# Window attention and a SoLU feed-forward block: plain float32 products of the first tiles from unsplit weights, and a start cut into halves

## The chip, the core and the metric

The kernel runs on one core of a Trainium2 chip. It is measured in microseconds of device time; the figure before the change is the median of three runs, 604.48 us (603.85 to 604.65). The engines are named as in the profile: PE multiplies matrices (PEld is its loading of the stationary operand), DVE, ACT and POOL work elementwise, and SP only issues transfers here.

## What is computed

The reference has two parts. Attention: 8 batches, 8 heads, 576 positions, 64 columns a head; every position sees itself and the 63 before it.

```python
scores = scale * np.matmul(q, k.transpose(0, 1, 3, 2))
mask = (rel >= 0) & (rel < window)              # window = 64
attn = softmax of the masked scores             # sum + 1e-9 below
x = np.matmul(attn, v)                          # 4608 tokens x 512
```

The feed-forward block on these 4608 rows, with `w_in` 512x1024 and `w_out` 1024x512:

```python
h = x @ w_in
sm = softmax(h)
solu = h * sm
ln = (solu - mean) / np.sqrt(var + 1e-6) * g_ln
out = ln @ w_out
```

The two weights are drawn as float64 (8 bytes a number), so the kernel reads 4 MB for each and turns the pairs of 32-bit words into float32 itself.

## The kernel before

The tokens are cut into 36 tiles of 128. For each tile `t` the work is the same:

- `load` (L296 to L317): q, k and two halves of v come in by transfers that SP issues.
- `scores` (L322 to L344): 16 small float32 products on PE into `pS`. `softmax` (L346 to L373): eight DVE operations add the mask and find the maxima, eight ACT operations take the exponential (`sS`, sums in `sm`), DVE makes reciprocals, and POOL multiplies the eight heads (L371).
- `transposes` (L378 to L394): eight PE transposes into `t`, copied to `PT` by ACT (first four heads) and DVE (the others).
- `values` (L405 to L419): 16 small float32 products into `pX`. ACT copies `pX` to `xH` in a reduced float32 format (fp32r), and DVE writes the rest, `xL = pX - xH`.
- `moe_in` (L429 to L437): `pH = x @ w_in` in two column halves. Each 128x512 product is made of three in fp32r: `xH*w_inH`, `xH*w_inL` and `xL*w_inH`, so 12 PE products a half and 24 a tile. There is one `pH` buffer, so the products of tile `t+1` wait until the norm of tile `t` has read it.
- `moe_norm` (L439 to L473): a maximum on DVE (L449), exponential on ACT (L451), product and sum on DVE (L454), square on ACT (L460), small columns on DVE and POOL, and two scalings of `e` on POOL (L471).
- `moe_transpose` and `moe_out` (L481 to L516): eight transposes of `e`, the copies `yH` and `yL`, 24 products into `pO` in the same three-part form, a copy to `ot` and a transfer out.

Before use, each of 16 blocks of weights, 128x512 each, is decoded (`weight_block`, L234 to L270): a transfer of 512 KB into `raw`, one ACT operation (L256), four DVE operations (L257, L259, L261, L263), for `w_out` a scaling by `g` on POOL (L266), a copy to the high part on ACT (L268), and the subtraction for the low part on POOL (L269). In the names of the trace `wt` is the block being decoded.

No engine chooses its order at run time. The functions above only record operations in a `Plan`, each with an engine, an estimated cost, what it reads and what it writes. `Plan.order` (L99 to L145) gives every operation a due time from the order in which PE's work was recorded, and then builds one list: at each step the engine that can begin first takes, of its ready operations, the one that is due first. Buffers are rings (`RINGS`, L33): an operation on buffer `n` waits for all users of the one that had its place. The order of PE is exactly the recorded order. The recording at the end of the function sets it: first the loads and weights of the start, then for each `t` the products of tile `t`, the transposes of `t+1`, the scores of `t+3` (`AHEAD`) and the output products of `t-3` (`BEHIND`).

Of the kernel before, what the change touches and what calls it, by code (L numbers as in the profile page):

```python
# [17 lines left out]
P = 128  # L18
# [8 lines left out]
BEHIND = 3  # L27

URGENT = 300
# [4 lines left out]
    "raw": 4, "wt": 3, "q": 3, "k": 3, "v0": 4, "v1": 4, "sS": 3, "PT": 2, "xH": 2, "xL": 2,  # L34
# [5 lines left out]
class Plan:  # L40
# [55 lines left out]
    def order(self):  # L96
# [32 lines left out]
        while any(waiting.values()):  # L129
# [21 lines left out]
def tile_window_attention_solu_moe(  # L151
# [15 lines left out]

    nc = tc.nc
# [9 lines left out]
    NTILE = NT // P  # L178
    SCALE = 1.0 / math.sqrt(D)
# [54 lines left out]
    def weight_block(i, src, wH, wL, g, key):  # L234


        n = wH.shape[-1]

        def raw():
            return T("raw", i, [P, n, 2], I32)  # L240

        def t():
            return T("wt", i, [P, n], I32)

        def tf():
# [9 lines left out]
        plan.dma(P * n * 8, lambda: nc.sync.dma_start(raw().rearrange("p n w -> p (n w)"), src), [], [R])
        plan.op("ACT", 600, lambda: nc.scalar.activation(tf(), hi().bitcast(F32), AF.Abs), [R], [W])  # L256
        plan.op("DVE", 420, lambda: nc.vector.tensor_scalar(  # L257
            tf(), tf(), EXP_LO, EXP_HI, ALU.max, ALU.min), [W], [W])
        plan.op("DVE", 420, lambda: nc.vector.tensor_scalar(  # L259
            t(), t(), 0x07FFFFFF, 3, ALU.bitwise_and, ALU.logical_shift_left), [W], [W])  # L260
        plan.op("DVE", 680, lambda: nc.vector.scalar_tensor_tensor(  # L261
            t(), hi(), -0x40000000, t(), ALU.bitwise_and, ALU.bitwise_or), [R, W], [W])
        plan.op("DVE", 680, lambda: nc.vector.scalar_tensor_tensor(  # L263
            t(), lo(), 29, t(), ALU.logical_shift_right, ALU.bitwise_or), [R, W], [W])
# [4 lines left out]
        plan.op("POOL", 1300, lambda: nc.gpsimd.tensor_sub(wL, tf(), wH.bitcast(F32)),  # L269
                [W, ("H", *key)], [("L", *key)])  # L270
# [321 lines left out]
```

## Time and profile before

| | us |
|---|---|
| median of three runs | 604.48 |
| the profiled execution, whole | 604.69 |
| its span (first to last instruction) | 602.5 |
| PE busy in the span | 563.9 |
| DVE busy | 322.0 |
| ACT busy | 313.3 |
| POOL busy | 210.2 |
| PE busy from 0 to 20 us | 1.98 |
| PE busy from 100 to 500 us | 400.0 |

The whole execution is 2.19 us longer than the span. In the tables by stretch, the first number behind the stretch is its length, and then come the busy time of PE, PEld, DVE, ACT and POOL with the number of instructions, the granted clock of PE, the busy share of the transfer engines and GB/s. In a timeline row the first number is the start, the second how long it took; what stands in brackets is how long the engine had been idle before, and what it waited for. Matmuls overlap, so the distance between two starts, not the length of one, is what a product costs PE. In the chain of waits the second number is the time that a piece adds to the chain.

### The profile page before, as it was taken

To read this page: it belongs to the slowest core of one execution; us is meant where nothing else is said; L and a number is where in the kernel's file an instruction comes from. 1 tells how busy PE (TensorE), PEld (TensorE's weight loads), DVE (VectorE), ACT (ScalarE), POOL (GpSimd) and SP (SyncE) were. 2 spreads that over 40 slices of the span, in tenths; PEclk is the share of its full clock that TensorE was granted. 3 is DMA by queue.
4 is the path that set the end of the run, shared out by engine and by line. 5 is a ranking of instruction groups with operands and counts; after the bars stand their busy time and mean duration, and the time that the engine had idled before them with its cause. 6 is when DMAs were issued, how large, how long until landed. Compare 5 with 4: busy or idle time off the path is not lost.

```text
span 602.5 us, 12551 instructions
## 1 busy us (share of the span) xinstructions
PE 563.9 (94%) x4608; PEld 459.3 (76%) x4608; DVE 322.0 (53%) x1180; ACT 313.3 (52%) x933; POOL 210.2 (35%) x438
## 2 busy tenths in 40 slices
PE   1387699999999999999999999999999999999997
PEld 1256578888888888888888888888888888888775
DVE  6768997555555555555555555555555555554430
ACT  3467666555555555555555555555555555553421
POOL 4554668333333333333333333333333333331110
PEclk9988889999999999999999999999999999999999
DMA  8882753333333333333333333333333331000000
GB/s 296 254 262 93 204 157 95 92 91 97 93 95 98 95 97 97 94 93 96 89 98 97 96 97 97 97 97 97 97 97 97 97 97 54 18 18 18 18 36 35
DMA packets 56204, 60.97 MB, mean 101 GB/s; under 512 B 3408, under 2 KB 40272, under 8 KB 56144
## 3 DMA queue, kind: packets, MB, share of 16 engines
q1 hardware_dynamic: 56144, 60.18, 32.7%
q8 instruction: 36, 0.59, 0.4%
q14 instruction: 24, 0.20, 0.1%
HBM read 50.73 MB, written 9.44 MB: 100 GB/s over the span
## 4 chain that ended last, share of the span: by engine, by line
PE 90%; DVE 5%; ACT 2%; POOL 1%; DMA 1%; issue 1%; SPq 0%; ACTq 0%
PE pO L508 35%; PE pH L434 34%; PE pX L411 6%; PE t L387 6%; PE pS L340 5%; PE t L491 5%; DVE wt L261 1%; DMA raw<-w_in 1%; DVE wt L263 1%; DVE sS L353 1%; DVE e L454 1%; POOL sS L371 1%; ACT sS L358 1%; POOL w_inL L269 0%; DVE wt L259 0%
## 5 line engine op out<-in xcount | busy, mean ns | idle before, releaser
L371 POOL TENSOR_SCALAR sS<-sS,rec 128x128 f32<-128x128 f32 x288 | 105.0, 386 | 258.6 <-PE pO L508 257.1
L358 ACT ACTIVATE sS<-sS,nmx 128x128 f32<-128x128 f32 x288 | 112.3, 391 | 52.9 <-DVE nmx L353 52.9
L434 PE MATMUL pH<-w_inH,xH 128*128 128x512 f32 x288 | 119.2, 414 | 8.6 <-DVE mst L454 8.6
L508 PE MATMUL pO<-w_outH,yH 128*128 128x512 f32 x288 | 117.7, 409 | 1.2 <-ACT yH L495 1.2
L434 PE MATMUL pH<-w_inH,xL 128*128 128x512 f32 x288 | 116.3, 404 | 0.0
L434 PE MATMUL pH<-w_inL,xH 128*128 128x512 f32 x288 | 116.0, 403 | 0.0
L508 PE MATMUL pO<-w_outH,yL 128*128 128x512 f32 x288 | 114.3, 397 | 0.0
L508 PE MATMUL pO<-w_outL,yH 128*128 128x512 f32 x288 | 113.9, 395 | 0.0
L495 ACT CAST yH<-t 128x512 fp32r<-128x512 f32 x72 | 38.7, 589 | 101.6 <-PE t L491 101.6
L449 DVE TENSOR_REDUCE mst<-pH 128x1 f32<-128x1024 f32 x36 | 44.1, 1224 | 70.5 <-PE pH L434 70.5
L392 DVE COPY PT<-t 128x512 f32<-128x512 f32 x36 | 24.9, 691 | 89.5 <-PE t L387 89.5
L434 PEld LDWEIGHTS pH<-w_inH,xH 128*128 128x128 f32 x288 | 55.3, 192 | 21.0 <-DVE mst L454 5.8
L471 POOL TENSOR_SCALAR e<-e,mst 128x512 f32<-128x512 f32 x72 | 54.9, 769 | 41.3 <-DVE mst L468 39.9
L508 PEld LDWEIGHTS pO<-w_outH,yH 128*128 128x128 f32 x288 | 54.1, 188 | 18.5 <-ACT e L451 4.8
L434 PEld LDWEIGHTS pH<-w_inH,xL 128*128 128x128 f32 x288 | 55.4, 192 | 13.5 <-DVE xL L418 0.2
L508 PEld LDWEIGHTS pO<-w_outH,yL 128*128 128x128 f32 x288 | 54.1, 188 | 14.6 <-DVE yL L497 1.7
L434 PEld LDWEIGHTS pH<-w_inL,xH 128*128 128x128 f32 x288 | 55.5, 193 | 11.7
L508 PEld LDWEIGHTS pO<-w_outL,yH 128*128 128x128 f32 x288 | 54.2, 188 | 11.6 <-POOL w_outL L269 0.2
L392 ACT COPY PT<-t 128x512 f32<-128x512 f32 x36 | 21.1, 585 | 76.5 <-PE t L387 76.5
L353 DVE CUSTOM_DVE_ANT_0 sS<-pS,maskNone 128x128 f32<-128x128 f32 x224 | 51.3, 286 | 14.0 <-PE pS L340 14.0
L387 PE MATMUL t<-ident,sS 128*128 128x128 f32 x288 | 42.0, 283 | 12.9 <-POOL sS L371 12.7
L358 ACT ACTIVATION_READ_ACCUMULATOR sS<-sS,nmx 128x1 f32 x288 | 53.9, 187 | 0.0
(54 smaller groups left out, 722.1 us busy)
## 6 DMA issues: line engine op xcount, KB each, us to landing
v<-vS SPq DMA_DIRECT2D x64, 256.0 KB, 4.1
k<-kT SPq DMA_DIRECT2D x35, 384.0 KB, 4.0
q<-qT SPq DMA_DIRECT2D x36, 256.0 KB, 4.6
y<-ot SPq DMA_DIRECT2D x36, 256.0 KB, 2.0
raw<-w_in SPq DMA_DIRECT2D x8, 512.0 KB, 5.2
raw<-w_out SPq DMA_DIRECT2D x8, 512.0 KB, 5.2
v<-vS SPq DMA_DIRECT2D x16, 128.0 KB, 4.5
k<-kT SPq DMA_DIRECT2D x1, 256.0 KB, 7.8
```

The source lines that it names most:

```text
L340: nc.tensor.matmul(PS(t)[half * WIN:(half + 1) * WIN, r, p], q[rs, p, half * WIN:(half + 1) * WIN], keys, start=True, stop=True)
L353: plan.op("DVE", 215, lambda h=h: nc.vector.tensor_tensor_reduce(SS(t)[:, h], PS(t)[:, h % 2, h // 2], mk, scale=-SCALE, scalar=BIG, op0=A ...
L358: plan.op("ACT", 390, lambda h=h: nc.scalar.activation(SS(t)[:, h], SS(t)[:, h], AF.Exp, bias=cols("nmx", h), scale=-1.0, accum_out=cols(" ...
L371: plan.op("POOL", 360, lambda h=h: nc.gpsimd.tensor_scalar(SS(t)[:, h], SS(t)[:, h], rec()[:, h:h + 1], 0.0, ALU.mult, ALU.add), [("rec", ...
L387: nc.tensor.transpose(pA()[:, i], SS(t)[:, 4 * x + i], ident)
L392: (nc.vector.tensor_copy if x else nc.scalar.copy)(PT(t)[:, 4 * x:4 * x + 4], pA()),
L411: nc.tensor.matmul(PX(t)[r * D:(r + 1) * D, p, ks], V(t, half)[:, h * D:(h + 1) * D], PT(t)[:, h, ks], start=True, stop=True)
L434: plan.op("PE", 233, lambda c=c, k=k, x=x, w=w: nc.tensor.matmul(PH(t)[:, hs], x(t)[:, c], w[:, c, hs], start=(c == k == 0), stop=(c == NC ...
L449: plan.op("DVE", 1150, lambda: nc.vector.tensor_reduce(nmax(), PH(t), axis=AX.X, op=ALU.max, negate=True), [("pH", t)], [key(0)])
L471: plan.op("POOL", 770, lambda h=h, hs=hs: nc.gpsimd.tensor_scalar(E(t)[:, hs], E(t)[:, hs], nmean(), kk(), ALU.add, ALU.mult), [key(4), ke ...
L495: plan.op("ACT", 560, lambda hs=hs, pT=pT: nc.scalar.copy(YH(t)[:, hs], pT()), [("t", n)], [("yH", t, h)])
L508: plan.op("PE", 233, lambda f=f, k=k, y=y, w=w: nc.tensor.matmul(PO(), y(t)[:, f], w[:, f], start=(f == k == 0), stop=(f == NF - 1 and k = ...
```

## The change

The weights of the first tiles are no longer split before they are used.

- Products. For tiles 0 to 2 `moe_in` multiplies `xH`, now a plain float32 copy of `pX`, by the decoded but unsplit weights `w` in plain float32: 8 products a tile, one per 128-row chunk and column half, in place of 24. For tile 0 `moe_out` does the same with `w_out`, 8 products. Tile 3 is the first to use split weights in `moe_in` (`PLAIN_IN`), tile 1 in `moe_out` (`PLAIN_OUT`); the split (`split`) is recorded there. `xL` and `yL` of the plain tiles fall away.
- Weights. They come in 8 chunks of 128x1024 (1 MB of raw words) with one set of decoding operations each; the first chunk comes as two halves. A chunk of `w_in` now holds both column halves of 128 rows, so the first products need the first chunk alone. The scaling by `g` moves from POOL to ACT, and the subtraction for the low part from POOL to DVE. Decoded chunks and low parts share a ring `w` of 9 places: a low part takes the place of a decoded chunk whose users are done.
- Attention of the first tiles. The scores are recorded as two operations of two head pairs each; for tile 0 the reciprocals come in two halves and the eight multiplications are on DVE, not POOL. For tiles 0 to 2 both copies to `PT` are on ACT (`EARLY`), and `values` and the copy to `xH` come in halves.
- Order. `BEHIND` goes from 3 to 2, with the `e` ring (`BEHIND + 1`) following. SP's transfers keep the recorded order, as PE's work does (`last`), except that operations of tile 0 marked `loose` may move on PE. q and k of tile 0 are recorded first. The planner's costs of transfers and weights change, and it adds 90 ns between dependent operations of one engine other than PE. `URGENT`, which nothing used, goes.

```diff
 AHEAD = 3
-BEHIND = 3
+HASTE = 1
+LOOSE = 1
+BEHIND = 2
+EARLY = 3
+PLAIN_IN = 3
+PLAIN_OUT = 1
...
-    "raw": 4, "wt": 3, "q": 3, "k": 3, "v0": 4, "v1": 4, "sS": 3, "PT": 2, "xH": 2, "xL": 2,
+    "raw": 3, "w": 9, "q": 3, "k": 3, "v0": 3, "v1": 3, "sS": 3, "PT": 2, "xH": 2, "xL": 2,
...
-            if engine == "PE":
-                if pe is not None:
-                    before[i].setdefault(pe, False)
-                pe = i
+            if engine in last and not loose:
+                if last[engine] is not None:
+                    before[i].setdefault(last[engine], False)
+                last[engine] = i
...
+        for x in (0, 1) if i == 0 else (slice(0, 2),):
+            n = 512 if i == 0 else 1024
...
         if g is not None:
-            plan.op("POOL", 700, lambda: nc.gpsimd.tensor_scalar(
-                tf(), tf(), g, 0.0, ALU.mult, ALU.add), [W, ("g",)], [W])
-        plan.op("ACT", 600, lambda: nc.scalar.copy(wH, tf()), [W], [("H", *key)])
-        plan.op("POOL", 1300, lambda: nc.gpsimd.tensor_sub(wL, tf(), wH.bitcast(F32)),
-                [W, ("H", *key)], [("L", *key)])
+            for x in range(2):
+                plan.op("ACT", 600, lambda x=x: nc.scalar.mul(tf()[:, x], tf()[:, x], g(x)),
+                        [("g",), W], [("w", i, x)])
...
+    def split(i):
+        for x in range(2):
+            plan.op("ACT", 600, lambda x=x: nc.scalar.copy(WH(i, x), W32(i)[:, x]),
+                    [("w", i), ("w", i, x), ("w", NC + 1 if i < NC else NW - 1)], [("H", i, x)])
+            plan.op("DVE", 620, lambda x=x: nc.vector.tensor_sub(
+                WL(i)[:, x], W32(i)[:, x], WH(i, x).bitcast(F32)),
+                [("w", i), ("w", i, x), ("H", i, x)], [("w", NW + i, x)])
...
+        if t < PLAIN_IN:
+            for c in range(NC if h == 0 else 0):
+                for x in range(2):
+                    plan.op("PE", 930, lambda c=c, x=x: nc.tensor.matmul(
+                        PH(t)[:, x * 512:(x + 1) * 512], XH(t)[:, c], W32(c)[:, x],
+                        start=(c == 0), stop=(c == NC - 1)),
+                        [("xH", t, c // 2), ("w", c), ("w", c, x)], [("pH", t)])
+            return
...
+    load(0, range(2))
+    prep(0)
     scores(0)
     softmax(0)
+    load(0, range(2, 4))
+    prep(1)
     load(1)
+    prep(2)
     transposes(0)
     scores(1)
     softmax(1)
     values(0)
+    prep(3)
     load(2)
...
+            if t - BEHIND == PLAIN_OUT:
+                for i in range(NC, NC + NF // 2):
+                    split(i)
+            on(moe_out, t - BEHIND)
```

How PE begins. Before: scores of tile 0, its transposes, scores of tile 1, values of tile 0, scores of tile 2, then the three-part products of the first column half.

```order
L340 MATMUL pS_158<-k_133,q_141 64x128 x16
L387 MATMUL t_231<-ident,sS_176 128x128 x4
L387 MATMUL t_245<-ident,sS_176 128x128 x4
L340 MATMUL pS_252<-k_155,q_204 64x128 x16
L411 MATMUL pX_274<-PT_239,v_0_221 64x64 x2
...
L340 MATMUL pS_321<-k_250,q_292 64x128 x16
L434 MATMUL pH_342<-w_inH,xH_306 128x512
L434 MATMUL pH_342<-w_inL,xH_306 128x512
L434 MATMUL pH_342<-w_inH,xL_313 128x512
```

Now, at the same place (`w_148`, `w_185`, `w_268` and `w_286` are the four chunks of `w_in`):

```order
L371 MATMUL pS_117<-k_112,q_110 64x128 x16
L425 MATMUL t_187<-ident,sS_134 128x128 x4
L425 MATMUL t_201<-ident,sS_134 128x128 x4
L449 MATMUL pX_210<-PT_199,v_0_138 64x64 x2
...
L371 MATMUL pS_220<-k_176,q_172 64x128 x16
L481 MATMUL pH_240<-w_148,xH_229 128x512 x2
L449 MATMUL pX_210<-PT_199,v_0_138 64x64 x2
...
L481 MATMUL pH_240<-w_185,xH_229 128x512 x2
L481 MATMUL pH_240<-w_268,xH_229 128x512 x2
L481 MATMUL pH_240<-w_286,xH_229 128x512 x2
```

The first chunk's products now stand between the two halves of tile 0's values, and the scores of tile 2 behind the last chunk.

The same stretch on ACT, where the weights' first operation (L279, out of `raw`) stands among the exponentials (L391) and the two copies of tile 0's `xH` (L459):

```order
L391 ACTIVATE sS_134,sm_142<-sS_134,nmx_135 128x128 x4
L279 ACTIVATE w_185<-raw_155 128x1024
L430 COPY PT_199<-t_187 128x512
L430 COPY PT_199<-t_201 128x512
L459 COPY xH_229<-pX_210 128x256
L391 ACTIVATE sS_242,sm_249<-sS_242,nmx_243 128x128
L459 COPY xH_229<-pX_210 128x256
L391 ACTIVATE sS_242,sm_249<-sS_242,nmx_243 128x128
L279 ACTIVATE w_268<-raw_207 128x1024
L391 ACTIVATE sS_242,sm_249<-sS_242,nmx_243 128x128 x5
L279 ACTIVATE w_286<-raw_247 128x1024
```

Before, the copies to `w_inH` of the first four blocks stood ahead of tile 0's exponentials; now no such copy stands in this stretch, and the third chunk (`w_268`) comes behind the second copy of `xH`, which waits for PE.

Where PE's output products begin. Before, the first product of `pO` comes behind the fourth tile's `pH` (`pH_811`, tile 3):

```order
L434 MATMUL pH_811<-w_inH,xH_793 128x512
...
L491 MATMUL t_889<-ident,e_482 128x128 x4
...
L340 MATMUL pS_926<-k_667,q_683 64x128 x16
L508 MATMUL pO_951<-w_outH,yH_903 128x512
```

Now it comes behind the third tile's `pH` (`pH_574`, tile 2), in plain float32, and the products of tile 3 (`pH_760`) follow it:

```order
L481 MATMUL pH_574<-w_286,xH_567 128x512 x2
L425 MATMUL t_617<-ident,sS_423 128x128 x4
...
L549 MATMUL t_633<-ident,e_366 128x128 x4
...
L371 MATMUL pS_671<-k_522,q_505 64x128 x16
L570 MATMUL pO_698<-w_315,yH_640 128x512 x2
L570 MATMUL pO_698<-w_354,yH_640 128x512 x2
L570 MATMUL pO_698<-w_480,yH_640 128x512 x2
L570 MATMUL pO_698<-w_551,yH_640 128x512 x2
L492 MATMUL pH_760<-w_inH,xH_684 128x512
```

From there to the end each `t` has the same sequence on PE as before, with output products one tile nearer. After the last `pH` (tile 35) three output tiles follow, where four did before.

More of the change, by code (lines that the diff above doesn't have):

```diff
@@ L326, in scores, with emit @@
         first = first_of(t)
-        def emit():
+        def emit(ps=range(NPAIR)):
             q, k = Q(t), K(t)
-            for p in range(NPAIR):
+            for p in ps:
                 for half in range(2):
@@ L364, in rec @@
             return T("rec", t, [P, H], pool=st)
[L366 to L373 removed]
+        engine, v, cost = ("POOL", nc.gpsimd, 360) if t else ("DVE", nc.vector, 150)
+        n = H if t else H // 2
+        for o in range(0, H, n):
+            s = slice(o, o + n)
+            R = ("rec", t, o)
+            plan.op("DVE", 130, lambda s=s: nc.vector.tensor_scalar_add(
+                rec()[:, s], T("sm", t, [P, H], pool=st)[:, s], 1e-9),
+                [("sm", t, h) for h in range(o, o + n)], [R])
+            plan.op("DVE", 130, lambda s=s: nc.vector.reciprocal(rec()[:, s], rec()[:, s]), [], [R])
+            for h in range(o, o + n):
+                plan.op(engine, cost, lambda h=h: v.tensor_scalar(
+                    SS(t)[:, h], SS(t)[:, h], rec()[:, h:h + 1], 0.0, ALU.mult, ALU.add),
+                    [R], [("sS", t, h)])
     def PT(t):
@@ L387, in emit @@
                     nc.tensor.transpose(pA()[:, i], SS(t)[:, 4 * x + i], ident)
-            plan.op("PE", 430, emit, [("sS", t, 4 * x + i) for i in range(4)], [("t", n)])
+            plan.op("PE", 430, emit, [("sS", t, 4 * x + i) for i in range(4)], [("t", n)], loose=t < LOOSE)
             plan.op(
-                "DVE" if x else "ACT", 600, lambda x=x, pA=pA:
-                (nc.vector.tensor_copy if x else nc.scalar.copy)(PT(t)[:, 4 * x:4 * x + 4], pA()),
+                "DVE" if x and t >= EARLY else "ACT", 600, lambda x=x, pA=pA:
+                (nc.vector.tensor_copy if x and t >= EARLY else nc.scalar.copy)(PT(t)[:, 4 * x:4 * x + 4], pA()),
                 [("t", n)], [("PT", t, x)])
@@ L404, in values, with emit @@
     def values(t):
-        def emit():
-            for p in range(NPAIR):
+        def emit(ps=range(NPAIR)):
+            for p in ps:
                 for half in range(2):
@@ L413, in emit @@
                             PT(t)[:, h, ks], start=True, stop=True)
-        plan.op("PE", 1100, emit, [("PT", t, x) for x in range(2)]
-                + [(f"v{half}", t, x) for half in range(2) for x in range(2)], [("pX", t)])
+        vals = [(f"v{half}", t, x) for half in range(2) for x in range(2)]
+        if t < PLAIN_IN:
+            for x in range(2):
+                ps = slice(2 * x, 2 * x + 2)
+                plan.op("PE", 550, lambda x=x: emit((2 * x, 2 * x + 1)), [("PT", t, x)] + vals, [("pX", t, x)],
+                        loose=t < LOOSE)
+                plan.op("ACT", 360, lambda ps=ps: nc.scalar.copy(XH(t)[:, ps], PX(t)[:, ps]),
+                        [("pX", t, x)], [("xH", t, x)])
+            return
+        plan.op("PE", 1100, emit, [("PT", t, x) for x in range(2)] + vals, [("pX", t)])
         plan.op("ACT", 560, lambda: nc.scalar.copy(XH(t), PX(t)), [("pX", t)], [("xH", t)])
@@ L494, in moe_transpose @@
             plan.op("PE", 430, emit, [("e", t, h)], [("t", n)])
+            if t < PLAIN_OUT:
+                plan.op("DVE" if h else "ACT", 600, lambda h=h, hs=hs, pT=pT:
+                        (nc.vector.tensor_copy if h else nc.scalar.copy)(YH(t)[:, hs], pT()),
+                        [("t", n)], [("yH", t, h)])
+                continue
             plan.op("ACT", 560, lambda hs=hs, pT=pT: nc.scalar.copy(YH(t)[:, hs], pT()),
```

194 lines of the change are left out of this document (108 added, 86 removed).

## The prediction

> **What bounds the kernel now.** I read the page first, then busy time by stretch, then the chain of waits, and last the timelines of the stretch that turned out to matter. The page's slices (40 of 15 us) and the stretches:
>
> ```profile
> span 602.5 us, 12551 instructions
> PE   1387699999999999999999999999999999999997
> DVE  6768997555555555555555555555555555554430
> ```
> ```profile
> 0.00:20.00 20.00, 1.98 (x32) 1.61 (x32) 14.55 (x35) 8.38 (x19) 8.88 (x22) 1.00 0.89 287
> 20.00:40.00 20.00, 12.89 (x125) 8.31 (x126) 15.32 (x52) 12.18 (x46) 11.31 (x20) 1.00 0.82 251
> 40.00:60.00 20.00, 17.00 (x173) 13.35 (x172) 13.96 (x41) 11.71 (x36) 10.33 (x20) 0.83 0.40 138
> 60.00:80.00 20.00, 14.36 (x108) 11.34 (x109) 18.48 (x61) 13.34 (x44) 13.78 (x18) 0.85 0.80 240
> 206.50:221.75 15.25, 15.25 (x130) 12.59 (x129) 7.74 (x31) 8.15 (x25) 4.86 (x11) 1.00 0.32 96
> ```
>
> PE is full from the sixth slice on, one tile taking 15.25 us with DVE and ACT half idle. Nothing there can be hidden better. Time is lost before 90 us, where DVE, at 14.6 and 18.5 of 20 us, is the busier engine. The chain says what PE did there (the second number is the time added):
>
> ```profile
> 44.47 1.10 PE pX L411 x32
> 48.95 4.51 PE pH L434 x12
> 76.08 4.45 PE pH L434 x12
> 85.30 1.08 PE pX L411 x32
> 86.38 1.03 PE pS L340 x32
> 87.41 5.80 PE pO L508 x24
> 93.21 2.80 PE pH L434 x12
> 96.02 0.87 PE t L387 x8
> ```
> ```profile
> 11.39 1.98 PE L340 MATMUL pS<-k,q 64*64 64x128 f32 x32 [11.39 <-DMA q<-qT]
> 32.80 0.50 PE L434 MATMUL pH<-w_inH,xH 128*128 128x512 f32 x1
> 41.28 0.63 PE L434 MATMUL pH<-w_inH,xH 128*128 128x512 f32 x1
> 41.70 0.63 PE L434 MATMUL pH<-w_inL,xH 128*128 128x512 f32 x1
> 48.95 0.50 PE L434 MATMUL pH<-w_inH,xH 128*128 128x512 f32 x1 [2.36 <-DVE mst L454]
> ```
>
> At 93.21 us PE has done `pO` of tile 0, `pH` of tiles 0 to 3 (5.60 each), `pX` and `t` of five tiles and `pS` of seven: 5.80 + 22.4 + 5.4 + 4.35 + 7.2, and 0.87 for `t` of `e`, 46.0 us. So 47.2 us are lost, in three ways. PE's first product of `pH` starts at 32.80, behind the weights. After each `pH` PE waits until the norm's L454 has read it (2.36 us idle at 48.95). And after such gaps come stretches at 0.43 us a product (41.28 to 41.70) in place of 2.80/12 = 0.233, with the granted clock at 0.83.
>
> **The change, part by part.** First the plain product, which the trace does not show at this size. The nearest rows are `pS` and `pX`, which are float32. Each is 16 products in the code, but 32 records, two per product, where the three-part products have one. From below, two records at 0.233 are 0.47 us. From above: `pS` has 64x64 operands, so four can lie side by side, 1.03/4 = 0.26 per 128 columns, and 1.03 for 512. `pX` (two side by side) gives 1.08/8 = 0.135 per 64 columns; the line through both gives 0.99 for 512. Small shapes carry more fill, so I take 0.95, near the upper rows: 7.6 us for eight products against 5.60, 2.0 more for each of three `pH` and one `pO`.
>
> The Trainium skill, "FP8 and Floating Point Precision", section TensorE Precision Notes, says that true FP32 takes four passes through the array. An estimate by it is 4 x 0.233 = 0.93, and the sum would be 0.5 us shorter; the two records per product don't contradict it.
>
> Now the weights and DVE. Durations, minimum, median and maximum:
>
> ```profile
> L256 ACT ACTIVATE wt<-raw x16: 650/666/697, 4.0 to 78.6; 128x512 f32<-128x512 f32 x16
> L257 DVE TENSOR_SCALAR wt<-wt x16: 418/424/1178, 4.7 to 82.3; 128x512 f32<-128x512 f32 x16
> L259 DVE TENSOR_SCALAR wt<-wt x16: 376/427/882, 5.2 to 83.2; 128x512 int32<-128x512 int32 x16
> L261 DVE SCALAR_TENSOR_TENSOR wt<-raw,wt x16: 680/693/1778, 5.6 to 84.1; 128x512 int32<-128x512 int32 x16
> L263 DVE SCALAR_TENSOR_TENSOR wt<-raw,wt x16: 676/691/1730, 6.4 to 87.6; 128x512 int32<-128x512 int32 x16
> L269 POOL TENSOR_TENSOR w_inL<-wt,w_inH x8: 1264/1288/1407, 7.9 to 39.7; 128x512 fp32r<-128x512 f32 x8
> ```
> ```profile
> 44.51 1.23 DVE L449 TENSOR_REDUCE mst<-pH 128x1 f32<-128x1024 f32 x1 [2.81 <-PE pH L434]
> 46.83 0.28 DVE L353 CUSTOM_DVE_ANT_0 sS<-pS,maskNone 128x128 f32<-128x128 f32 x1
> 47.03 0.29 DVE L353 CUSTOM_DVE_ANT_0 sS<-pS,maskNone 128x128 f32<-128x128 f32 x1
> 47.66 1.22 DVE L454 CUSTOM_DVE_ANT_0 e<-pH,e 128x1024 f32<-128x1024 f32 x1
> 48.12 0.40 ACT L358 ACTIVATE sS<-sS,nmx 128x128 f32<-128x128 f32 x1
> 48.50 0.40 ACT L358 ACTIVATE sS<-sS,nmx 128x128 f32<-128x128 f32 x1
> ```
>
> A half block costs DVE 2.4 us with the gaps. For a 1024-wide chunk the bounds are twice the 512 medians, 4.5, and the 1.22 of L454 for the last two with half as much for the first two, 3.7; I take 4.0. DVE gains 16 subtractions (0.68, like L261) and tile 0's eight multiplications (0.2, between mask and half a half block), 12.5 us; it loses the stretching to 1.7 us that L261 and L263 show at their maximum, as long as L269 on POOL, which is gone.
>
> ```profile
> 0.73 1.81 SPq L255 DMA_DIRECT2D raw<-w_in  x4
> 3.11 0.67 SPq L300 DMA_DIRECT2D q<-qT  x1
> 4.02 0.66 ACT L256 ACTIVATE wt<-raw 128x512 f32<-128x512 f32 x1 [2.02 <-DMA raw<-w_in]
> ```
>
> q and k, now issued first, land some 3.3 us behind an issue at 0.73 and 1.4 (the first `raw` took that): 5.2, not 11.39. At 287 GB/s the chunks land at about 6, 8, 12, 18 and 21 us, always ahead of DVE. From there, in the new order:
>
> - `pS` of tile 0, at half pace, 5.2 to 7.2; eight masks at 0.21 to 8.1; the first chunk's halves (4.8), tile 0's reciprocals (0.8) and multiplications (1.6) on DVE to 15.3; transposes, copies, the first half of `pX` and `pS` of tile 1 to 18.7; first-chunk products, partly at half pace, 20.9; the other half of `pX` 22.0.
> - DVE has chunk 2 at 19.5. Its chunk 3 waits for L279 on ACT, which is queued behind the second `xH` copy (22.5) and an exponential: 24.0, then 4.0 each and 0.4 for reciprocals, so chunk 3 at 28.0 and chunk 4 at 32.4. The last two plain products end at 35.0, partly at half pace.
> - Gap 1: L449 to 36.3, tile 2's masks 1.7, two weight operations 1.5, L454 to 40.8. PE has `pS`, `t`, `pS`, `pX` inside, 4.0 us. `pH` of tile 1: 40.8 + 7.6 + 1.7 for one slow stretch (7 or 8 products at 0.2 more, as around 41 us) = 50.1.
> - Gap 2: L449, two weight operations, L454 to 54.3, the `xH` copy behind weights on ACT to 54.9. `pH` of tile 2: 54.9 + 7.6 + 1.7 = 64.2.
> - L449 and the `PT` copy on DVE 66.1, `pX` and `pS` 68.2, `pO` of tile 0 to 75.9. One more for POOL's multiplications beside DVE, as L257's maximum of 1.18 shows: 76.9.
>
> At that point PE owes one `pH`, `pS`, `t` and `pX` more than at 93.21 before (the output comes one tile earlier): 5.60 + 1.03 + 0.87 + 1.08 = 8.58. Its equal is 84.63, so the start gains 84.63 - 76.9 = 7.7 us. The split casts and subtractions behind it (eight of each, 5 us, against 7 idle us a tile on both engines) are covered by `pO` and `pH`; uncovered they would cost that 5 us.
>
> `BEHIND` also shortens the end:
>
> ```profile
> 584.08 1.04 PE L491 MATMUL t<-ident,e 128*128 128x128 f32 x8
> 591.37 1.03 PE L491 MATMUL t<-ident,e 128*128 128x128 f32 x8
> 219.93 1.52 POOL L471 TENSOR_SCALAR e<-e,mst 128x512 f32<-128x512 f32 x2 [1.33 <-DVE mst L468]
> ```
>
> Output tiles there take 7.29 for 0.87 + 5.80 of work: 0.62 of waiting each, three times and not four. In the steady tiles `e` of the tile whose `pH` ended at 206.5 is ready at 221.5; its transposes come two periods behind 206.5, at 237, so 15 us are left. Sum: 602.5 - 7.7 - 0.6 = 594.2. The profiled execution is 2.19 longer than its span and 0.21 above the median: 594.2 + 2.19 - 0.21 gives 596.2 us, 1.4% faster.
>
> **Rivals.**
>
> - *DVE's floor.* From 6.3 on DVE owes, until tile 3: chunks 33, masks of five tiles 8.5, norms 3 x 3.4, `w_in` subtractions 5.4, tile 0's 2.4, small ones 3, about 62: 68. For it: PE's work to there is 45 us, and slow stretches may fail to come. Against it: DVE waits for PE at three places above. Time 596.2 - 8.9 = 587.3.
> - *DVE held by POOL.* Multiplications on POOL beside 28 weight operations; if eight stretch by 1.0 as L261 did, the start ends at 85: 604. For it: the maxima; against it: those came beside L269, which is gone.
> - *A slow feed.* 512-byte rows of q, k and v delay the chunks, since three, not four, `raw` buffers (of 1 MB) hold SP back: 251 GB/s puts chunk 4 three us later and with the wait two more, 601.
> - *Half pace throughout (slower).* The plain products are spread over gaps. If `pH` of tiles 1 and 2 and `pO` of tile 0 all run at 0.43/0.233 of their time, 24 x 0.95 x 0.85 = 19.4 less the 3.4 counted, 16.0 more: 612.2. It decides from five slow stretches more than I count (8.3 us). For it: four slow stretches between 40 and 81 us; against it: each lasted about 3 us though PE idled between.
>
> The Trainium skill, "TensorE: Matmul & The Clock Gate", section "The HAM clock gate", has the clock halve after an idle window of about 3.4 us. The 2.36 us gap here was enough to be followed by a slow stretch, so the trace disagrees in size; by the page's figure both counted stretches (3.4 us) would fall away.
>
> **How the numbers follow.** Forecast 0.50, DVE's floor 0.22, POOL 0.13, slow feed 0.07, half pace 0.08. The plain product's bounds move 24 products on the path: at 1.03 by +1.9, at 0.47 by -11.5, which DVE's floor stops at 587.3. The range holds that floor and the slow feed, and leaves out the half pace and the upper half of POOL's case: 586.5 to 603.5. About 0.2% (1.2 us) is what a measurement here can tell from no change. Faster 0.86 (forecast, floor, feed, half of POOL), same 0.05, slower 0.09.
>
> **What would show it.** `pS` of tile 0 near 5, a first plain `pH` product near 19, the four chunks' products spread to about 35, `pO` of tile 0 ahead of tile 3 and ending near 77, two records per plain product 0.47 apart, a steady tile still 15.25, and three output tiles after the last `pH`. Wrong would be: idle PE ahead of `t` of `e` in steady tiles, a chunk's L279 waiting for its transfer, or slow plain products in all three batches.

## The result, and the profile after

The changed kernel takes 594.17 us (median of four runs, 593.86 to 595.72), the kernel before 604.57 beside it (603.85 to 605.14): a ratio of 0.9839, with a 95% interval of 0.9824 to 0.9854, or 1.6% faster. The prediction was 596.2. The profiled execution took 593.86, its span 592.1, 10.4 less than the 602.5 before.

The page of the kernel after, span and slices (40 of 14.8 us), answers to the first rows shown of before:

```profile
span 592.1 us, 12478 instructions
PE   2689899999999999999999999999999999999997
DVE  4889985554444444554444455555455555554330
```

The stretches of the kernel after (columns as before: length, busy PE, PEld, DVE, ACT, POOL, the granted clock, transfer share, GB/s):

```profile
0.00:20.00 20.00, 8.29 (x90) 5.96 (x91) 11.06 (x42) 8.41 (x24) 3.62 (x18) 1.00 0.90 304
20.00:40.00 20.00, 14.50 (x136) 7.34 (x134) 16.36 (x48) 11.06 (x31) 5.11 (x8) 0.83 0.84 294
40.00:60.00 20.00, 18.82 (x109) 9.49 (x110) 19.12 (x59) 19.28 (x55) 13.60 (x19) 1.00 0.69 204
60.00:80.00 20.00, 17.98 (x123) 12.32 (x122) 18.50 (x52) 17.33 (x53) 7.68 (x11) 0.91 0.25 74
206.50:221.75 15.25, 15.25 (x130) 12.57 (x129) 7.82 (x32) 8.27 (x26) 4.86 (x11) 1.00 0.32 94
```

PE is full from the sixth slice on, as before, but has 2, 6, 8 and 9 tenths in the first four slices where it had 1, 3, 8 and 7. A steady tile still takes 15.25 us of nothing but PE. Between 40 and 60 us DVE is busy for 19.1 of 20 and ACT for 19.3: the gaps there are filled on three engines at once. Of the chain of waits the output products and the end:

```profile
67.49 7.06 PE pO L570 x16
84.00 5.81 PE pO L580 x24
...
560.87 5.64 PE pH L492 x24
...
582.31 6.14 PE pO L580 x24
```

`pO` of tile 0 ends at 67.49 + 7.06 = 74.55. The equal point before was 84.63, so the start gains 10.1; behind it come 592.1 - 74.55 = 517.55 us, with three output tiles behind the last `pH`. The start on PE, from the timeline (start, length, in brackets the idle time before and what ended it; a plain product has two records):

```profile
4.93 1.98 PE L371 MATMUL pS<-k,q 64*64 64x128 f32 x32 [4.93 <-DMA k<-kT]
17.47 1.99 PE L371 MATMUL pS<-k,q 64*64 64x128 f32 x32
19.39 1.98 PE L481 MATMUL pH<-w,xH 128*128 128x512 f32 x4
...
27.94 6.41 PE L481 MATMUL pH<-w,xH 128*128 128x512 f32 x8 [4.04 <-DVE w L287]
40.06 7.13 PE L481 MATMUL pH<-w,xH 128*128 128x512 f32 x16 [0.47 <-ACT xH L459]
52.61 7.10 PE L481 MATMUL pH<-w,xH 128*128 128x512 f32 x16 [0.58 <-ACT xH L459]
59.55 1.04 PE L425 MATMUL t<-ident,sS 128*128 128x128 f32 x8
61.17 0.63 PE L549 MATMUL t<-ident,e 128*128 128x128 f32 x4 [0.59 <-ACT PT L430]
63.24 0.63 PE L549 MATMUL t<-ident,e 128*128 128x128 f32 x4 [1.43 <-DVE PT L430]
63.79 1.98 PE L449 MATMUL pX<-PT,v 128*64 128x64 f32 x32
65.70 1.79 PE L371 MATMUL pS<-k,q 64*64 64x128 f32 x32
```

Tiles 1 and 2 run at full pace: eight plain products in 7.1 us. The slow places are others: the third and fourth chunk of tile 0 (6.41 for four products), and `pX` and `pS` at 63.8 (1.98 and 1.79, where 1.15 and 1.10 are usual). And ahead of `pO` PE waits twice for copies to `PT`, one on ACT, one on DVE. DVE at that place:

```profile
60.15 1.21 DVE L287 SCALAR_TENSOR_TENSOR w<-raw,w 128x1024 int32<-128x1024 int32 x1
61.28 1.21 DVE L507 TENSOR_REDUCE mst<-pH 128x1 f32<-128x1024 f32 x1
62.42 0.67 DVE L430 COPY PT<-t 128x512 f32<-128x512 f32 x1
```

The copy of the second half of tile 3's `PT` stands behind a weight operation and a norm, and the transposes of `e` need the `t` buffer that it reads.

Ahead of 32 us the weights reach DVE through ACT. ACT's and DVE's rows for chunk 2, then DVE's for chunk 3:

```profile
14.75 1.14 ACT L279 ACTIVATE w<-raw 128x1024 f32<-128x1024 f32 x1 [2.08 <-DMA raw<-w_in]
15.93 0.69 DVE L281 TENSOR_SCALAR w<-w 128x1024 f32<-128x1024 f32 x1 [0.44 <-ACT w L279]
23.85 0.69 DVE L281 TENSOR_SCALAR w<-w 128x1024 f32<-128x1024 f32 x1 [1.41 <-ACT w L279]
```

Chunk 2 landed at 14.7, and its first operation waited 2.08 us for the transfer. DVE had other work and lost only 0.44 us by it. Chunk 3's L279 stood on ACT behind the second copy of `xH`, as the prediction has it, and DVE idled 1.41 us for it.

### The profile page after: what moved, and what is told of

It reads as the page before. It is cut to its first block, busy times and chain, and to the rows that moved or that the text cites. A ratio compares the mean times of both kernels' runs of the same rounds, so it can differ in the third digit from the quotient of the medians.

```text
span 592.1 us, 12478 instructions
## 1 busy us (share of the span) xinstructions
PE 567.1 (96%) x4576; PEld 451.3 (76%) x4576; DVE 318.0 (54%) x1171; ACT 321.6 (54%) x939; POOL 186.9 (32%) x406
## 4 chain that ended last, share of the span: by engine, by line
PE 90%; DVE 3%; DMA 3%; ACT 2%; SPq 1%; issue 1%; ACTq 0%
PE pO L580 35%; PE pH L492 31%; PE pX L449 7%; PE pS L371 6%; PE t L549 5%; PE t L425 5%; DMA raw<-w_in 2%; PE pO L570 1%; DMA k<-kT 1%; DVE w L285 1%; PE pH L481 1%; DVE w L287 1%; ACT sS L391 0%; SPq L343 0%; ACT w L279 0%
## 5 line engine op out<-in xcount | busy, mean ns | idle before, releaser
L391 ACT ACTIVATE sS<-sS,nmx 128x128 f32<-128x128 f32 x288 | 112.3, 392 | 41.8 <-DVE nmx L386 41.8
L580 PE MATMUL pO<-w,yH 128*128 128x512 f32 x280 | 111.2, 397 | 0.0
L492 PE MATMUL pH<-w_inH,xH 128*128 128x512 f32 x264 | 107.7, 408 | 0.0
L492 PE MATMUL pH<-w_inH,xL 128*128 128x512 f32 x264 | 103.7, 393 | 0.0
L492 PE MATMUL pH<-w,xH 128*128 128x512 f32 x264 | 103.4, 395 | 0.0
L507 DVE TENSOR_REDUCE mst<-pH 128x1 f32<-128x1024 f32 x36 | 44.1, 1225 | 74.1 <-PE pH L492 72.0
L580 PEld LDWEIGHTS pO<-w,yH 128*128 128x128 f32 x280 | 52.6, 188 | 10.5
L492 PEld LDWEIGHTS pH<-w_inH,xL 128*128 128x128 f32 x264 | 49.6, 188 | 12.3 <-issue 0.2
L492 PEld LDWEIGHTS pH<-w_inH,xH 128*128 128x128 f32 x264 | 49.6, 188 | 10.9 <-ACT w_outH L306 0.2
L492 PEld LDWEIGHTS pH<-w,xH 128*128 128x128 f32 x264 | 49.7, 188 | 10.0
L391 ACT ACTIVATION_READ_ACCUMULATOR sS<-sS,nmx 128x1 f32 x288 | 53.9, 187 | 0.0
L560 DVE TENSOR_TENSOR yL<-t,yH 128x512 fp32r<-128x512 f32 x70 | 44.8, 681 | 7.7 <-ACT yH L558 7.7
L371 PE MATMUL pS<-k,q 64*64 64x128 f32 x1152 | 42.2, 287 | 5.9 <-DMA k<-kT 4.9
```

Of the source, the lines that this page charges most:

```text
L371: nc.tensor.matmul(PS(t)[half * WIN:(half + 1) * WIN, r, p], q[rs, p, half * WIN:(half + 1) * WIN], keys, start=True, stop=True)
L391: plan.op("ACT", 390, lambda h=h: nc.scalar.activation(SS(t)[:, h], SS(t)[:, h], AF.Exp, bias=cols("nmx", h), scale=-1.0, accum_out=cols(" ...
L492: plan.op("PE", 233, lambda n=n, c=c, x=x, w=w: nc.tensor.matmul(PH(t)[:, hs], x(t)[:, c], WH(c, h) if w is WH else WL(c)[:, h], start=(n ...
L507: plan.op("DVE", 1150, lambda: nc.vector.tensor_reduce(nmax(), PH(t), axis=AX.X, op=ALU.max, negate=True), [("pH", t)], [key(0)])
L560: plan.op("DVE", 620, lambda hs=hs, pT=pT: nc.vector.tensor_sub(YL(t)[:, hs], pT(), YH(t)[:, hs].bitcast(F32)), [("t", n), ("yH", t, h)], ...
L580: plan.op("PE", 233, lambda f=f, i=i, x=x, k=k, y=y, w=w: nc.tensor.matmul(PO(), y(t)[:, f], w(i, x), start=(f == k == 0), stop=(f == NF - ...
```

## The experiments

Each time is a median; the kernel before was run beside each and stood between 604.4 and 605.0.

### What the plain products are worth

First all products three-part again, by the change's own two numbers:

```diff
-PLAIN_IN = 3
-PLAIN_OUT = 1
+PLAIN_IN = 0
+PLAIN_OUT = 0
```

> No plain products: every tile uses the three-part products, so all of w_in is split before the first pH; chunks, halves, first q and k, and BEHIND 2 stay. My theory (the split kept the first products back): the first pH waits for eight copies on ACT and eight subtractions on DVE behind the decode, so that pH of tile 0 ends near 45 to 47 in place of 34.4; 32 products at 0.87 become triples at 0.70, which gives 5.4 us back; net 4 to 8 us slower than the changed kernel, 598 to 602. Rival (early q and k, halves and BEHIND carry the gain, the plain products only cost PE 5.4 us more): 588 to 593.

610.91 us (610.58 to 611.24), ratio to before 1.0113 [1.0097, 1.0129]: slower even than the kernel before, and far above the 598 to 602 expected. Two rows of PE's timeline, then two of DVE's:

```profile
37.60 0.80 PE L492 MATMUL pH<-w_inH,xH 128*128 128x512 f32 x1 [16.60 <-ACT w_inH L306]
43.63 0.80 PE L492 MATMUL pH<-w_inH,xH 128*128 128x512 f32 x1 [3.77 <-ACT w_inH L306]
```
```profile
38.34 1.28 DVE L287 SCALAR_TENSOR_TENSOR w<-raw,w 128x1024 int32<-128x1024 int32 x1
39.54 1.28 DVE L308 TENSOR_TENSOR w<-w,w_inH 128x512 fp32r<-128x512 f32 x2
```

PE idles 16.6 us, and the first subtraction begins at 39.54, when DVE has decoded six chunks, two of them of `w_out`. That is not the price of three-part products. In the plan `split` of `w_in` names the second chunk of `w_out` (`NC + 1`) among its reads, and the ring rule lets the first user of a buffer begin no earlier than that of the buffer recorded before it, where the low parts are recorded behind all chunks. So in the lists of ACT and DVE the splits stand behind decoding of `w_out`, and PE waits for them. One of the two numbers alone shows the same rule:

```diff
-PLAIN_IN = 3
+PLAIN_IN = 1
```

> Only tile 0 takes plain products of w_in; tiles 1 and 2 take three-part ones, so the split of w_in (eight ACT casts of 0.67, eight DVE subtractions of 0.62) stands ahead of tile 1's pH. PE saves 2 x (7.0 - 5.6) = 2.8 us. Theory: DVE is the bound in the first 60 us, so 5 us of subtractions ahead of tile 1 cost more than PE saves, +2 to +5 against the change: 596 to 599. Rival: DVE and ACT do them in gaps that PE's norms leave anyway, and PE's saving counts: 591 to 593.

600.15 us (599.86 to 600.55), ratio 0.9933 [0.992, 0.9947], 6.0 slower than the change, one above the upper end of the theory. DVE's timeline, the first and the last mask of tile 2:

```profile
36.05 0.28 DVE L386 CUSTOM_DVE_ANT_0 sS<-pS,maskNone 128x128 f32<-128x128 f32 x1
...
42.13 0.28 DVE L386 CUSTOM_DVE_ANT_0 sS<-pS,maskNone 128x128 f32<-128x128 f32 x1
```

Between them stand five decoding operations of `w_out`, which the splits made urgent for the planner; the scores of tile 3 need the one `pS` buffer, and PE idles 6.2 us until 42.53. So a kernel was needed in which the products are three-part but the split isn't held. The ring gets 16 places, and the split is recorded where the chunks have come:

```diff
-PLAIN_IN = 3
-PLAIN_OUT = 1
+PLAIN_IN = 0
+PLAIN_OUT = 0
-    "raw": 3, "w": 9, ...
+    "raw": 3, "w": 16, ...
-                    [("w", i), ("w", i, x), ("w", NC + 1 if i < NC else NW - 1)], [("H", i, x)])
+                    [("w", i), ("w", i, x)], [("H", i, x)])
...
     prep(3)
+    for i in range(NC):
+        split(i)
...
-        if t == PLAIN_IN:
-            for i in range(NC):
-                split(i)
```

> All products are three-part ones again, as in the run with both plain counts at 0 (610.91 us), but without that run's ring rule: the ring of decoded chunks and low parts has 16 places, not 9, the split of w_in is recorded behind the fourth chunk and waits for no chunk of w_out, so each chunk is split when it is decoded. Theory: most of the 16.7 us by which that run was slower than the change came from splits held behind the decoding of w_out, not from the products. Here tile 0's pH ends near 40.7 us (chunk 3 at 31.7, six subtractions of 0.62 ahead, then pS and the second column half) where the change has 34.3 and a pS behind it, 5.3 later; tiles 1 and 2 take 1.4 us less each and tile 0's output 1.2 less, and the subtractions for w_out, 5 us on DVE, come ahead of that output, of which up to 3 show: +1.5 to +4.5, 595.5 to 598.5. Rival: the plain products themselves are what the change gains, and the time stays above 603.

596.46 us (596.3 to 596.99), ratio 0.9867 [0.9848, 0.9887]; the theory holds. PE's timeline:

```profile
34.01 0.80 PE L492 MATMUL pH<-w_inH,xH 128*128 128x512 f32 x1 [2.86 <-ACT w_inH L306]
42.09 1.03 PE L425 MATMUL t<-ident,sS 128*128 128x128 f32 x8
70.98 0.50 PE L580 MATMUL pO<-w_outH,yH 128*128 128x512 f32 x1
76.70 0.40 PE L492 MATMUL pH<-w_inH,xH 128*128 128x512 f32 x1
```

`pH` of tile 0 ends at 42.09 in place of 34.28, but three-part products of tiles 1 and 2 and the earlier split give most of it back: `pO` of tile 0 ends at 76.70, 2.15 behind the change's 74.55. The spans are 594.4 and 592.1, the medians 2.3 apart as well, and every run of this kernel is above every run of the change. By the two ratios, each to the kernel before beside it, the distance is 1.7 us, and their intervals just overlap. So of the change's 10.4 us the plain products, against this plan and given all the rest, are worth about 2. About eight come from the other parts: the order, the chunks, `BEHIND`, and what was moved between engines.

The traces show where these eight arise. At the end of tile 2's `pH` this kernel and the kernel before have done the same work on PE, at 67.90 and 70.52: 2.6 us. At the end of `pO` of tile 0 (76.70, the equal point before 84.63) it is 7.9. The 5.3 between come from one place of the kernel before:

```profile
76.08 0.47 PE L434 MATMUL pH<-w_inH,xH 128*128 128x512 f32 x1 [3.37 <-DVE mst L454]
```

There PE idles 3.37 us for the norm of tile 2, and the twelve products behind the gap take 4.45 in place of 2.80 (the prediction's chain). Here `t` of `e`, `pX`, `pS` and `pO` of tile 0 stand behind tile 2's `pH`, 8.8 us of work without a gap.

### One output tile earlier

```diff
-BEHIND = 2
+BEHIND = 3
```

> The changed kernel with BEHIND back at 3 and nothing else undone. My theory (the shorter distance gives 0.6 us at the end, and one gap before a pH that pO then covers): four output tiles follow the last pH again (+0.6), pO of tile 0 stands behind pH of tile 3, and PE idles once more, 1 to 3 us, before pH of tile 3: 595 to 598 us, span 1 to 4 us above 592.1. Rival (the distance matters at the end alone): +0.6, 594.8. Second rival (pO of tile 0 came too early for its weights and copies, as the 3.9 us of waits at 59.6 to 67.4 in the changed kernel say): at or below 594.2.

598.29 us (596.7 to 599.14), ratio 0.99 [0.9882, 0.9918]: 4.1 slower than the change, and just above the theory's 595 to 598. PE's timeline:

```profile
68.64 0.77 PE L492 MATMUL pH<-w_inH,xH 128*128 128x512 f32 x1 [1.88 <-ACT sS L391]
```

Without output products to do, PE waits 1.88 us. The profile names an exponential, but these products don't read what it writes; DVE's L512, which reads the one `pH` buffer, ended at 68.48, so it is the norm again that PE waits for. The products behind that gap start 0.43 us apart up to 71.87, not 0.233. The same number in the kernel before:

```diff
-BEHIND = 3
+BEHIND = 2
```

> The kernel before with BEHIND at 2 and nothing else. My theory (the earlier output products need the earlier weights of the change): 0.6 us less at the end, but pO of tile 0 now stands ahead of pH of tile 3 and waits for the low parts of w_out, whose last came at 91 us before; between 603 and 608, not faster than 603. Rival (the shorter distance by itself covers a gap of the start): 599 to 602.

602.73 us (601.88 to 604.7, ten runs), ratio 0.9981 [0.9968, 0.9994]: 1.7 faster by the medians, 1.1 by the ratio, so the theory of a loss fell, and the rival was a little too hopeful. PE's timeline inside `pO` of tile 0 shows why the gain is small there:

```profile
77.58 0.50 PE L508 MATMUL pO<-w_outH,yL 128*128 128x512 f32 x1 [0.86 <-DVE yL L497]
82.25 0.50 PE L508 MATMUL pO<-w_outL,yH 128*128 128x512 f32 x1 [0.86 <-POOL w_outL L269]
```

An earlier output in the old order waits for the split of `w_out` piece by piece. In the new one its products run without a gap (67.49 to 74.55); what waits there is the transposes of `e` ahead of them.

### Where the start's own pieces stand

The first chunk, and tile 0's reciprocals, in one piece:

```diff
-        for x in (0, 1) if i == 0 else (slice(0, 2),):
-            n = 512 if i == 0 else 1024
+        for x in (slice(0, 2),):
+            n = 1024
...
-        n = H if t else H // 2
+        n = H
```

> The first chunk in one piece as the others, and tile 0's reciprocals in one piece: the halves are undone (scores and values stay in two parts). My theory (the first half's early landing fills DVE from 9 us on): DVE idles about 2 us after the masks until the whole chunk has landed, and tile 0's transposes start later by 2 to 3 us: 595.5 to 597. Rival (the halves only cost extra instructions; DVE makes it up in its gaps at 19 and 23 us): 593.5 to 594.7.

592.70 us (590.89 to 594.76), ratio 0.9812 [0.9785, 0.984]. The theory, that the halves help, was wrong, and the time lies below the rival's 593.5 to 594.7 too. The first scores begin at 6.20, not 4.93, and the first transposes much later, but PE's timeline shows the third and fourth chunk's products not later:

```profile
16.67 1.09 PE L425 MATMUL t<-ident,sS 128*128 128x128 f32 x4 [8.49 <-DVE sS L409]
27.06 1.95 PE L481 MATMUL pH<-w,xH 128*128 128x512 f32 x4 [1.41 <-DVE w L287]
31.67 1.98 PE L481 MATMUL pH<-w,xH 128*128 128x512 f32 x4 [2.65 <-DVE w L287]
```

When the first piece starts doesn't set this 31.7. Mostly DVE's sum of work does: from its first mask to the end of chunk 4 DVE is busy for 21.2 of 24.6 us in the change and for 20.1 of 23.2 here. Most of the rest is waiting for L279, which on ACT waits for the work ahead of it or for its transfer. The second test says the same of q and k:

```diff
-    load(0, range(2))
     prep(0)
+    load(0, range(2))
```

> The first chunk of weights recorded ahead of q and k of tile 0, so both its halves are issued first. My theory (the first scores head the chain): pS of tile 0 starts 3 to 4 us later than 4.93, and the time grows by 1 to 3 us, 595 to 597, not by all of it, because DVE decodes the first chunk while it waits. Rival (DVE is the bound of the start, and any work it gets earlier is as good): no change or up to 2 us faster, 592 to 594.2.

592.86 us (588.71 to 594.43), ratio 0.9801 [0.9761, 0.984]; scores at 8.53, 3.6 later, and the end of tile 0's `pH` at 33.83, not later. The rival held. Neither the halves nor q and k in front bring time; both intervals touch the change's own, so that they cost any isn't shown. What the medians are lower by (1.5 and 1.3 us) needn't come from these edits as such: in both profiles `pX` and `pS` ahead of tile 0's output take 1.15 and 1.10, not 1.98 and 1.79, and the runs' mean granted clocks are 0.993 to 1.000, where all four runs of the change have 0.991.

### The subtractions on DVE or on POOL

```diff
-            plan.op("DVE", 620, lambda x=x: nc.vector.tensor_sub(
+            plan.op("POOL", 1300, lambda x=x: nc.gpsimd.tensor_sub(
```

> The 16 subtractions of the split on POOL, as before the change, not on DVE. My theory (POOL's subtraction, 1.3 us against 0.6 and stretching DVE's operations beside it, was a cost of the kernel before): L285, L287 or L386 beside it stretch to 1.2 to 1.7, pH of tile 3 waits for low parts, and the time is 0 to 4 us longer, 594.2 to 598. Rival (DVE is the bound of the start): 9.6 us of DVE's work are gone, and the time falls by 1 to 4 us, 590 to 593.

595.08 us (594.22 to 596.53), ratio 0.9851 [0.9829, 0.9872]: 0.9 slower than the change by the medians, as the theory has it, though the intervals overlap. The profile is of the slowest of its four runs (596.53). From the groups of the first 90 us (busy, then mean ns), and PE's timeline:

```profile
L308 POOL TENSOR_TENSOR w<-w,w_inH 128x512 fp32r<-128x512 f32 x8 | 13.3, 1682 | 0.2
```
```profile
65.44 1.59 PE L549 MATMUL t<-ident,e 128*128 128x128 f32 x8 [4.26 <-ACT PT L430]
```

One subtraction takes 1.68 us on POOL, 0.68 on DVE (the 5.3 us for eight in the change), and the wait ahead of tile 0's output doubles (2.02 in the change). Beside it DVE's L285 and L287 at 59.70 and 61.90 took 2.17 us each, 1.21 in the change, and the `PT` copy on ACT stood behind a weight operation that waited for the second of them.

### The slow products and the copies to PT

Nine unused plain products of 128x192 into the still unused `pO`, between the second and third chunk of tile 0, where PE otherwise idles. They are overwritten; nothing else is changed.

```diff
+                if t == 0 and c == 1:
+                    for _ in range(9):
+                        plan.op("PE", 0, lambda: nc.tensor.matmul(
+                            PO(0)[:, :P + WIN], ident, band, start=True, stop=True), [], [("pO", 0)])
```

> Nine idle products (128x192, into the pO buffer that nothing has used yet) on PE between the second and the third chunk of tile 0, where it idled from 23.9 to 27.9 us. My theory (half pace follows idle time): the last four plain products of tile 0 take 0.87 each in place of 1.58, pH of tile 0 ends 2.0 to 2.8 us earlier, and the time falls by 1.5 to 2.8, 591.4 to 592.7. Rival (slow stretches come at fixed times, whatever PE does): no change, 594.2, or a slow stretch elsewhere.

592.34 us (591.99 to 593.37), ratio 0.9808 [0.979, 0.9827], 1.8 faster than the change by the medians, the time that the theory gives. Two stretches of the change, then the same two of this kernel:

```profile
27.00:35.00 8.00, 7.00 (x34) 2.91 (x38) 5.87 (x9) 2.43 (x4) 5.11 (x8) 0.62 0.83 273
62.00:68.00 6.00, 4.76 (x70) 4.10 (x71) 6.00 (x13) 4.82 (x17) 0.00 (x0) 0.72 0.24 66
```
```profile
27.00:35.00 8.00, 5.02 (x42) 2.22 (x40) 6.49 (x9) 2.89 (x5) 5.08 (x8) 1.00 0.76 249
62.00:68.00 6.00, 4.99 (x74) 3.42 (x75) 6.00 (x13) 5.63 (x19) 0.00 (x0) 1.00 0.27 87
```

The granted clock is 1.00 in both, where it was 0.62 and 0.72. But the way is another than the theory's. In the first stretch the clock gives little, since the fourth chunk is decoded at 32.1 and `pH` of tile 0 ends at 34.09 (34.28 in the change), not 2.0 to 2.8 earlier. Slow products came ahead of it, as the rival allows: the first chunk's two took 3.11 us, not 1.98. Some 1.5 of the 1.8 us come from the second stretch, where `pX` and `pS` take 1.15 and 1.10.

Next, tile 3's second copy to `PT` on ACT as well:

```diff
-EARLY = 3
+EARLY = 4
```

> Tile 3's second PT copy on ACT too, not on DVE behind L287 and L507. My theory (that copy held PE from 61.8 to 63.8, and the idle time brought the slow pX and pS behind it): PE's wait before the second transposes of e shrinks by 1 to 1.5 us, and the time falls by 1 to 2.5, 591.7 to 593.2. Rival (ACT is as full there as DVE, 17 of 20 us, and yH or xH slips by as much): 593.7 to 594.7.

594.01 us (593.16 to 594.42), ratio 0.9829 [0.9811, 0.9846]: no gain, the rival's number. PE's timeline:

```profile
31.84 3.78 PE L481 MATMUL pH<-w,xH 128*128 128x512 f32 x4 [1.37 <-DVE w L287]
62.65 1.11 PE L549 MATMUL t<-ident,e 128*128 128x128 f32 x8 [0.58 <-ACT PT L430]
81.25 0.63 PE L549 MATMUL t<-ident,e 128*128 128x128 f32 x4 [1.42 <-DVE PT L430]
```

The wait of 1.43 at 63.24 is gone, and comes back as 1.42 at 81.25, at the copy of tile 4, which is still on DVE behind subtractions; the rival had ACT give it back. The slow stretch moved too: the fourth chunk's products took 3.78 us here, and `pH` of tile 0 ended 1.3 later than in the change, while `pX` and `pS` ahead of the output took 1.15 and 1.10, 1.5 less. Hence both repairs together, with tiles 3 and 4 on ACT:

```diff
-EARLY = 3
+EARLY = 5
+                if t == 0 and c == 1:
+                    for _ in range(9):
+                        ...
```

> Both repairs together: the nine unused plain products of 128x192 behind tile 0's second chunk (as run alone: 592.34 us) and both PT copies of tiles 3 and 4 on ACT (tile 3's alone: 594.01, since tile 4's copy on DVE then held PE 1.4 us). Theory: what is left in the 7.9 us ahead of tile 0's output is PT copies queued behind weight operations on DVE, 1.5 to 3 us of it; with both copies on ACT nothing gives it back later, so 589 to 591, and PE is at the first product of tile 3's pH by 70 to 71.5 us. Rival: ACT's queue, which then carries both halves of PT and sixteen weight operations a tile, holds PE as long as DVE did: 591.8 to 593, no change from the dummies alone.

591.08 us (589.55 to 591.23), ratio 0.9778 [0.9762, 0.9793]: the fastest of all kernels here, 3.1 us below the change and with an interval clear of the change's. PE's timeline:

```profile
61.48 1.11 PE L553 MATMUL t<-ident,e 128*128 128x128 f32 x8 [0.56 <-ACT PT L430]
...
71.21 0.80 PE L496 MATMUL pH<-w_inH,xH 128*128 128x512 f32 x1
```

The time is 0.1 above the theory's upper end, and tile 3's `pH` begins at 71.21, inside its 70 to 71.5. The same with the first chunk in one piece, and three unused products behind the second, six behind the third chunk:

```diff
-        for x in (0, 1) if i == 0 else (slice(0, 2),):
+        for x in (slice(0, 2),):
...
-EARLY = 3
+EARLY = 5
+                if t == 0 and c in (1, 2):
+                    for _ in range(3 * c):
+                        ...
```

> The first chunk and the first reciprocals in one piece (alone: 592.70 us), three unused plain products behind tile 0's second chunk and six behind its third, both PT copies of tiles 3 and 4 on ACT. Its profile without the other two had no slow pX or pS ahead of tile 0's output, so the unused products have little to give here. Theory: only the PT copies count, 588.5 to 591. Rival: DVE's operations are the bound in this order, 591.5 to 593. The unused products could cost up to 1 us where a chunk is ready before they end: 593 to 594.

592.58 us (590.11 to 592.81), ratio 0.9799 [0.9779, 0.9819]: the rival's range, and nothing over the whole chunk alone. PE's timeline:

```profile
20.80 3.78 PE L481 MATMUL pH<-w,xH 128*128 128x512 f32 x4 [0.47 <-ACT xH L459]
33.80 1.98 PE L481 MATMUL pH<-w,xH 128*128 128x512 f32 x4 [1.19 <-DVE w L287]
```

The first chunk's two products ran at half pace in this profile (3.78 us; 1.98 in the run with the chunk in one piece alone), and the fourth chunk was decoded 2.1 us later than there. The way from a slow PE at 21 us to DVE at 33 goes through ACT. The second half of `pX` came 2.1 us later than there (27.08 for 24.96), so did the copy to `xH` (27.82 for 25.70), and chunk 4's L279 stands behind that copy: DVE idled 2.77 us for it, where it had idled 0.21.

## Why the prediction came out right

The forecast and its mechanism held, with a span 2.1 us too long (594.2 for 592.1). The single steps, predicted and measured, in us from the span's start:

| step | predicted | measured |
|---|---|---|
| q and k land, first scores | 5.2 | 4.93 |
| tile 0's multiplications end | 15.3 | 15.4 |
| first plain products end | 20.9 | 21.3 |
| chunks 2, 3, 4 decoded | 19.5, 28.0, 32.4 | 20.9, 27.8, 31.7 |
| `pH` of tile 0 ends | 35.0 | 34.28 |
| gap 1, then `pH` of tile 1 | 5.8 + 9.3 | 5.78 + 6.97 |
| gap 2, then `pH` of tile 2 | 4.8 + 9.3 | 5.58 + 6.94 |
| from there to `pO` of tile 0 | 4.1 | 7.94 |
| `pO` of tile 0, with POOL's share | 8.6 | 7.06 |
| `pO` of tile 0 ends | 76.9 | 74.55 |
| from there to the end of the span | 517.3 | 517.55 |

So the sum is right to 0.4% partly by luck, since steps that were 7.0 us too long in all meet steps that were 4.9 too short:

- *The plain product* was taken as 0.95 and is 0.87 to 0.88 (6.97/8, 7.06/8): near the upper row, as argued, but 0.6 too long in each batch, 1.8 in all.
- *The two slow stretches* of 1.7 in `pH` of tiles 1 and 2 didn't come. Gap 1 has idle pieces of 0.99 and 0.47 us and gap 2 pieces of 0.45 and 0.58, the rest filled by transposes and scores; no 2.4 us gap like the one that preceded slow products before. Together 3.4 us too long.
- *From `pH` of tile 2 to `pO`* 4.1 was 3.8 too short. The step named the `PT` copy on DVE behind the norm's first operation, but let that begin at once; L507 began at 61.28, 1.7 us behind the last product, since L287 and a subtraction (said to be covered) were queued ahead of it on DVE. The transposes of `e` behind the copy, 0.6, weren't counted. The other 1.6 are `pX` and `pS` at a clock of 0.72: a slow stretch did come, at another place than either counted one. The runs with the unused products and with `EARLY` at 5 take these parts away one by one.
- *POOL's 1.0* was put at `pO`; nothing was slow there. What showed is 0.8 in gap 2, where DVE waited 0.79 for POOL's part of the norm and PE 0.45 for its multiplications.
- *The tail and the equal point* held within 0.25: 517.55 against 517.3. From the equal point before it is 517.87, so 0.3 of the 0.6 shows.

Of the rivals, *DVE's floor* is half true. DVE is what tile 0 waits for (4.04 us idle on PE ahead of chunk 3), and moving the start's scores, or cutting its first chunk, moves little; but the 587.3 us of that rival weren't reached by any kernel, 588.71 being the lowest single run. *The slow feed* didn't cost what it names: chunks 3 and 4 were earlier than forecast, with transfers at 294 to 304 GB/s. But a sign that the prediction named as wrong, a chunk's L279 waiting for its transfer, did show: chunk 2 landed at 14.7, not 12, and not ahead of DVE. It cost DVE 0.44 us, and PE 0.35 through the `PT` copies behind it on ACT. *Half pace throughout* fell: the three plain batches it named run at full pace, and the slow stretches cost 1.6 us at `pX` and `pS` and some 0.8 at tile 0's last products (chunk 4 is there at 31.7, and two products behind it would end at 33.4, not 34.28). Its sign, slower, was reached only with three-part products whose split was held.

By the rule cited of the Trainium skill's "TensorE: Matmul & The Clock Gate", section "The HAM clock gate" (a clock that halves behind an idle window of about 3.4 us), both counted stretches should fall away. They did, and behind 4.04 idle us the clock fell to 0.62, which agrees. The 0.72 between 62 and 68, behind idle pieces of 0.59 and 1.43, doesn't agree in size. By the four passes of the Trainium skill's "FP8 and Floating Point Precision", section TensorE Precision Notes, the prediction's estimate for the plain product was 0.93; it measured 0.87.

What the sum never asked is which part of the change earns the time. It priced the plain products at 2.0 us more of PE for each batch and took the late split for granted; against a plan that splits each chunk as it comes they earn only about 2 us of 10.4. How the other eight divide stays partly open. 5.3 arise where PE used to wait ahead of tile 3's `pH`; undoing `BEHIND` costs 4.1 in the new order (it gives 1.7 alone in the old, and the parts don't add up), the subtraction's move off POOL about 0.9, the halves and the place of q and k nothing that shows; the planner's costs and the new shape of the chunks weren't tried alone.

## What to carry to other kernels

Before an edit gets the credit for a gain, run its opposite with the plan free to fit: taking the plain products back cost 16.7 us where a buffer rule held the split that then came first, and about 2 where it didn't. Where an engine has work for most of a stretch, starting its first piece earlier or cutting it finer gave nothing here. The time lay in the order of its work: look for a short copy that another engine waits for, queued behind long work that nobody waits for yet, and try it on another engine. And a step whose wait is removed for one tile will wait at the next tile under the same rule, so take both.

## What the runs showed of the hardware that was not expected

- A plain float32 product of 128x512 takes 0.87 us, in two records, 3.7 times the 0.233 of an fp32r product, and below both figures worked out from the small products (0.99 and 1.03).
- Unused products at 24 to 27 us raised the granted clock not only in the stretch behind them (0.62 to 1.00) but also 35 us later (0.72 to 1.00), behind the same idle pieces of 0.58 and 1.43. All four runs of the change have a mean clock of 0.991, those of this kernel 0.997 to 1.000. Three of four runs with the first chunk whole have 1.000 without any unused product, so filling the gap isn't the only way there. What carries it over 35 us no run shows. The Trainium skill's "TensorE: Matmul & The Clock Gate", same section, has the window run free of the kernel's start, so that slow products may vary from run to run; the four runs of the change don't, those with q and k behind the weights do (0.994 to 1.000).
- The granted clock doesn't tell of all slow products: `pS` at 4.93 and 17.47 took 1.98 and 1.99, not 1.10, in a stretch whose clock reads 1.00.
